# Attention with a mixture layer in double-precision words: inputs laid out by the host in three new ways, four bit operations changed, the hand-written order replaced

## The chip, the cores and the metric

The kernel runs on one core of one Trainium2 chip. The metric is device time in microseconds, the median of several executions; the profile is one further execution of the same program, with its own time.

## The reference

```python
scores = q @ k^T / sqrt(64);  causal mask;  attn = softmax(scores)      # 4 batches x 12 heads, 448 positions, 64 wide
x = (attn @ v) laid out as 1792 tokens x 768
h = max(x @ w1, x @ w2, x @ w3)                                          # 768 x 768 each
out = h @ w_out                                                          # 1792 x 768
```

q, k and v are float32. The four weights come as 8-byte floating-point words (float64); each is read as pairs of 32-bit words, of which the upper word carries sign, exponent and the top of the mantissa.

## The kernel before

**Units.** Attention goes by 24 units u = 6b + p, a pair of heads p of a batch b. `staging` loads for a unit k and q, 128 x 448 float32 each (two heads above each other), and for every second unit a tile kx of 128 x 2 x 288: the last 64 queries and 224 keys of two units with the heads exchanged, in four transfers (line 693, two for q and two for k). `attend` computes a unit's scores in two halves into PSUM (a and b of the group names; line 720), takes row maxima on VectorE (L766), exponentials on ScalarE (L790), and brings the probabilities into position: for the first six units by transposes on TensorE (L804) with copies out of PSUM (L528 on ScalarE, L530 on VectorE), for the other 18 by splitting into two half-precision parts (cast L528 or L530, difference L539 on VectorE or GpSimd) and transposing by DMA on SP's queue (L859). Then come the products with v, 60 matmuls a unit in two halves (L884), scaling by the row sums and a split of the result x.

**Weights.** 24 weight tiles of 768 KB, m = 0 to 23, three to a group f. `weight` loads one (L981 for w1 to w3, six pieces of 1 KB for each partition; L985 for w_out, one piece of 6 KB), takes the absolute value of the upper words on ScalarE (L1015) and their clamped maximum on VectorE (L1000), and puts a float32 together out of the two words by bit operations (L1004, L1008, L1012). `scales` (group names c0 to c7) spreads the three maxima of a group to all partitions by matmuls (L567), takes the maximum (L572) and makes a power of two of it with L577, L583, L587 and a reciprocal (L595). `split` makes two half-precision parts with these factors (L528 or L530 or L532, and L548 or L550 and L551). There are two buffers for weight tiles as loaded, four for what is made of them.

**Layers.** `hidden` computes the first layer for batches 0 and 1 (L1092, three parts of six 448-column matmuls for each product, evicted by L1107), `project` the second (L1503). For batches 2 and 3 seven products take the place of eight (`seven`, L1324; `project_seven`, L1449), of combined weights and tokens.

**Order.** All operations are first listed with their readers and writers; `ORDER` gives the order in which they are placed and `ENGINE`, two letters for each, the engine or queue (pe, dv, ac, po, sp). Each engine then executes its own in that order, and waits at the first that isn't ready. The lists hold 1,940 operations. Loads are issued from SP's and ScalarE's queues, DMA transposes from SP's only. Buffers go round in rings (`RINGS`: two each of k and q, one kx).

Of the kernel before, what the change touches and what calls it, by code (L numbers as in the profile page):

```python
# [1642 lines left out]
```

## Time and profile before

| | us |
|---|---|
| median of 3 runs | 455.27 (453.88 to 458.81) |
| the profiled execution | 458.94 |
| its span, first to last instruction | 457.2 |
| TensorE busy in it | 435.9 |
| VectorE busy | 418.7 |
| ScalarE busy | 298.3 |
| GpSimd busy | 116.7 |
| mean granted TensorE clock | 0.984 |

A busy TensorE is not TensorE at its peak, since matmuls are pipelined and their ends modelled. PEld is the load of a matmul's stationary operand, which overlaps. Idle time of an engine that isn't the bottleneck costs nothing. A row of the timeline gives start, duration, engine, line and operation, out<-in with shapes, how often, and in brackets the idle time of the engine ahead of it and what ended that.

### The profile page before, as it was taken

The numbers are of one execution on the slowest core, as the hardware profiler recorded it, in microseconds if no ns is written. First come the engines' busy times: TensorE is split into PE (matmuls) and PEld (weight loads), VectorE is DVE, ScalarE is ACT, GpSimd is POOL, SyncE is SP. The second block draws the span as 40 slices with busy tenths as digits, with TensorE's granted clock in tenths as the row PEclk, the third lists the DMA queues.
The fourth block names the chain that finished last, engine by engine and source line by source line (L and its number), as shares of the span: only waits on it lengthen the run. The fifth ranks groups of instructions, "written<-read, shape, count | busy, mean of one in ns | idle before, by whom it ended". The sixth has DMA issues, their size and how long they took to land. (4 is left out here: it accounts for less than half of the span.)

```text
span 457.2 us, 11068 instructions
## 1 busy us (share of the span) xinstructions
PE 435.9 (95%) x4349; PEld 254.5 (56%) x4349; DVE 418.7 (92%) x835; ACT 298.3 (65%) x722; POOL 116.7 (26%) x118
## 2 busy tenths in 40 slices
PE   6789898999799999999999999999999999999996
PEld 3568674555365555555555566655555555555553
DVE  2989999999789998998798999899999999999994
ACT  2998989788586898997477788794333342431520
POOL 2025542333333414423200035111021203122010
PEclk9889999999889999999999999999999999999999
DMA  7958678999879868926898785873010000000024
GB/s 253 273 178 251 196 258 207 227 199 232 185 196 216 253 193 172 286 63 134 189 164 155 162 168 112 148 135 87 21 42 0 1 1 0 2 0 1 0 82 161
DMA packets 109235, 64.02 MB, mean 140 GB/s; under 512 B 80512, under 2 KB 106624, under 8 KB 109184
## 3 DMA queue, kind: packets, MB, share of 16 engines
q1 hardware_dynamic: 97504, 48.08, 46.6%
q10 hardware_dynamic: 11680, 15.24, 10.8%
q8 instruction: 34, 0.56, 0.5%
q14 instruction: 17, 0.14, 0.1%
HBM read 38.93 MB, written 5.51 MB: 97 GB/s over the span
## 5 line engine op out<-in xcount | busy, mean ns | idle before, releaser
L1092 PE MATMUL M<-x,w 128*128 128x448 f16 x648 | 129.2, 355 | 0.6 <-ACT region L528 0.5
L790 ACT ACTIVATE region<-S,acc 128x128 f32<-128x128 f32 (+3 forms) x168 | 81.5, 495 | 22.6 <-POOL acc L778 7.9
L1092 PEld LDWEIGHTS <-w 128*128 128x128 f16 x648 | 61.5, 98 | 58.0 <-issue 3.7
L766 DVE TENSOR_REDUCE acc<-S 128x2 f32<-128x768 f32 (+1 forms) x96 | 61.2, 665 | 12.7 <-PE S L720 10.4
L539 POOL TENSOR_TENSOR region<-region 128x1024 f16<-128x1024 f32 (+1 forms) x18 | 37.3, 2071 | 60.0 <-ACT region L1015 21.9
L720 PE MATMUL S<-region 64*64 64x224 f32 (+6 forms) x768 | 49.2, 367 | 2.1 <-DMA region<-in_k_dram 1.1
L528 ACT ACTIVATE region<-region,cols 128x384 f16<-128x384 f32 (+1 forms) x37 | 22.0, 612 | 43.0 <-DVE region L1182 33.5
L528 ACT ACTIVATE region<-region 128x1024 f16<-128x1024 f32 (+3 forms) x48 | 37.9, 798 | 17.3 <-DVE region L1257 7.8
L1324 PEld LDWEIGHTS <-region 128*128 128x128 f16 x324 | 31.7, 98 | 29.6 <-DVE region L548 0.2
L1177 POOL TENSOR_TENSOR region<-w 128x384 f32<-128x384 f16 x21 | 19.0, 911 | 106.6 <-DVE region L1177 36.4
L1503 PE MATMUL M<-h,w 128*128 128x448 f16 x216 | 42.6, 353 | 0.0
L720 PEld LDWEIGHTS S<-region 64*64 64x64 f32 x768 | 33.7, 139 | 7.2 <-issue 2.4
L1324 PE MATMUL L<-region,region 128*128 128x448 f16 x180 | 36.3, 352 | 0.0
L1324 PEld LDWEIGHTS <-w 128*128 128x128 f16 x243 | 23.5, 98 | 22.4 <-issue 0.7
L790 ACT ACTIVATION_READ_ACCUMULATOR region<-S,acc 128x1 f32 x168 | 34.3, 204 | 0.0
L1324 PE MATMUL M<-x,w 128*128 128x448 f16 x162 | 33.1, 353 | 0.5 <-DVE hacc L530 0.5
L1503 PEld LDWEIGHTS <-w 128*128 128x128 f16 x216 | 20.6, 98 | 20.0 <-issue 1.3
L884 PEld LDWEIGHTS <-region 128*64 128x64 f16 x1080 | 26.4, 111 | 6.6 <-issue 6.2
L528 ACT ACTIVATE region<-region,acc 128x128 f32<-128x128 f32 (+3 forms) x56 | 27.4, 524 | 3.9 <-PE S L720 2.1
L884 PE MATMUL O<-region,region 128*64 128x128 f16 (+1 forms) x1080 | 29.1, 211 | 0.0
L1015 ACT ACTIVATE region<-region 128x768 f32<-128x768 f32 x24 | 21.9, 914 | 8.3 <-DMA region<-in_moe_w_dram 8.3
L1000 DVE TENSOR_SCALAR_CACHE_REDUCE region<-region 128x768 f32<-128x768 f32 x24 | 22.7, 944 | 4.8 <-ACT region L1015 4.7
(180 smaller groups left out, 798.5 us busy)
## 6 DMA issues: line engine op xcount, KB each, us to landing
region<-in_moe_w_dram SPq DMA_DIRECT2D x9, 768.0 KB, 5.9
region<-in_moe_w_dram ACTq DMA_DIRECT2D x9, 768.0 KB, 5.5
region<-in_k_dram SPq DMA_DIRECT2D x20, 224.0 KB, 3.9
region<-in_v_dram SPq DMA_DIRECT2D x11, 384.0 KB, 4.3
region<-in_q_dram SPq DMA_DIRECT2D x17, 224.0 KB, 4.5
region<-in_moe_w_out_dram SPq DMA_DIRECT2D x4, 768.0 KB, 5.5
region<-in_k_dram SPq DMA_DIRECT2D x22, 112.0 KB, 3.3
out_dram<-osb ACTq DMA_DIRECT2D x8, 224.0 KB, 2.5
```

The costliest lines, as they stand in the source:

```text
L528: ACT.activation(o, i, AF.Copy, scale=f)
L539: ENG[eng].tensor_tensor(out=o, in0=i, in1=hi, op=ALU.subtract)
L720: PE.matmul(ap(o, 512 * h + dims[0], dims[1:], D * g, D), l, r, start=start, stop=True, skip_group_check=True)
L766: DVE.tensor_reduce(out=ap(T(acc), at, [[4, len(g)]]), in_=i, op=ALU.max, axis=AX.XY if parts == 2 else AX.X, negate=True)
L790: ACT.activation(o, part(T(S), parts, c, w), AF.Exp, bias=T(acc)[:, 16 + at : 17 + at], scale=0.125, accum_out=T(acc)[:, 8 + at : 9 + at])
L884: PE.matmul(T(O)[D * h : D * h + D, P * i : P * i + w], vt[j][:, vl, (2 * p + h) * D : (2 * p + h + 1) * D], queries(T(pT[u]), i, h, 8 * p ...
L1000: DVE.tensor_scalar(out=T(x32), in0=T(x32), scalar1=MIN_HI, scalar2=None, op0=ALU.max, op1=ALU.max, accum_out=wmx[:, c])
L1015: add([("act", c_act(DM, 0.025))], lambda e: ACT.activation(T(x32), word(1).bitcast(F32), AF.Abs), reads=[st], writes=[x32], ring=("w3", x ...
L1092: PE.matmul(T(M)[:, 0:S_LEN], w16[j][:, kk, wl, fs], xx[:, kk % 3, xl], start=(kk == 0 and wl + xl == 0), stop=(kk == 5 and wl == 1))
L1177: add(c_add(n), lambda e: ENG[e].tensor_tensor(out=o(), in0=a()[0], in1=a()[1], op=ALU.add), reads=reads, writes=writes, ring=ring, prio=p ...
L1324: PE.matmul(T(M)[:, 0:S_LEN], stat(c, wl), mov(c, xl), start=first and n == 0, stop=n == 8, skip_group_check=True)
L1503: PE.matmul(T(M)[:, 0:S_LEN], w16[3][:, f, wl, es], T(("h", b, f))[:, hl], start=(f == 0 and hl + wl == 0), stop=(f == 5 and wl == 1))
```

## The change

The host, which already transposed q, k and v, lays the inputs out anew: q and k of a unit stand beside each other in one row of 896; the contents of kx stand as rows of 576 in a tensor of its own (`cross`); w1 to w3 stand tile by tile, each partition's 6 KB in one piece. So a unit's q and k are one transfer of 448 KB into one tile qk (ring of two), kx is one of 288 KB instead of four, and a weight tile has rows of 6 KB instead of six of 1 KB. The bytes are the same.

The upper words are scaled by 2^16 in the ScalarE operation that takes their absolute value. `power` (L577) goes: `exponent` does the shift and the mask in one instruction. `low30` (shift and mask) becomes `shift`, `top2` becomes `sign`, with another constant.

The two lists are replaced. They hold 1,908 operations: 24 fewer for q, 8 fewer for `power`. Before, 387 are on TensorE, 755 on VectorE, 575 on ScalarE with its queue, 102 on GpSimd and 121 on SP's queue (where one operation for kx issues four transfers); now 387, 723, 579, 110 and 109.

```diff
-TOP2 = -0x40000000
-LOW30 = 0x3FFFFFFF
+SIGN = -0x80000000
-MIN_HI = 2.0**-15 * 1.125
+MIN_HI = 2.0 * 1.125
...
-ORDER = [16, 15, 17, 18, 941, 19, 30, 49, 20, 50, 0, 31, 2, 21, 32, 33, 22, 23, 24, 942, 26, 25, 34, 943, 4, 6, 35, 944,
+ORDER = [15, 17, 18, 917, 16, 48, 923, 19, 29, 20, 918, 919, 0, 30, 21, 2, 4, 22, 23, 6, 7, 24, 49, 31, 32, 33, 80, 920,
...
-    qr=2, kr=2, xr=1, kx=1, acc=2, p32=2, ph=2, pT=3, v16=5, vr=4, w3=4, x=4, wst=2, h=6, hacc=4, osb=2, S=2, O=1, M=3,
+    qk=2, xr=1, kx=1, acc=2, p32=2, ph=2, pT=3, v16=5, vr=4, w3=4, x=4, wst=2, h=6, hacc=4, osb=2, S=2, O=1, M=3,
...
-        def power(e):
-
-            DVE.tensor_scalar(
-                out=at(1).bitcast(I32), in0=at(0).bitcast(I32), scalar1=3, scalar2=TOP2, op0=ALU.logical_shift_left,
-                op1=ALU.bitwise_xor)
-
         def exponent(e):
-            k = int(shifted)
-            DVE.tensor_scalar(
-                out=at(k + 1).bitcast(I32), in0=at(k).bitcast(I32), scalar1=EXP32, scalar2=None, op0=ALU.bitwise_and)
+            if shifted:
+                DVE.tensor_scalar(
+                    out=at(1).bitcast(I32), in0=at(0).bitcast(I32), scalar1=3, scalar2=EXP32, op0=ALU.logical_shift_left,
+                    op1=ALU.bitwise_and)
+            else:
+                DVE.tensor_scalar(
+                    out=at(1).bitcast(I32), in0=at(0).bitcast(I32), scalar1=EXP32, scalar2=None, op0=ALU.bitwise_and)
...
+        def both_of(e):
+            ENG[e].dma_start(T(qk), both_[b, p * P : (p + 1) * P, :])
 
         def other(e):
-            for x, w, at in ((q, D, 0), (k, 224, D)):
-                for h in range(2):
-                    r, c = p * P + D * (1 - h), 224 * h if at else 384
-                    i = bass.AP(x.tensor, x[b, r : r + 1, c : c + 1].offset, [[S_LEN, D], [P * S_LEN, 2], [1, w]])
-                    ENG[e].dma_start(T(kx)[D * h : D * h + D, :, at : at + w], i)
...
+            r = (6 * b + p) // 2 * P
+            ENG[e].dma_start(T(kx).rearrange("p a b -> p (a b)"), cross[r : r + P, :])
...
         def ld(e):
-            if m < 18:
-                ENG[e].dma_start(
-                    stage().rearrange("p (a f) -> p a f", a=KC),
-                    wi[j][:, f * 256 : (f + 1) * 256].rearrange("(a p) f -> p a f", p=P))
-            else:
-                ENG[e].dma_start(stage(), wi[3][f * P : (f + 1) * P, :])
+            ENG[e].dma_start(stage(), wi[j][f * P : (f + 1) * P, :])
...
-        def low30(e):
-            DVE.tensor_scalar(
-                out=xi(), in0=xi(), scalar1=3, scalar2=LOW30, op0=ALU.logical_shift_left, op1=ALU.bitwise_and)
+        def shift(e):
+            DVE.tensor_scalar(out=xi(), in0=xi(), scalar1=3, scalar2=None, op0=ALU.logical_shift_left)
...
-        def top2(e):
+        def sign(e):
             DVE.scalar_tensor_tensor(
-                out=xi(), in0=word(1), scalar=TOP2, in1=xi(), op0=ALU.bitwise_and, op1=ALU.bitwise_or)
+                out=xi(), in0=word(1), scalar=SIGN, in1=xi(), op0=ALU.bitwise_and, op1=ALU.bitwise_or)
...
-        add([("act", c_act(DM, 0.025))], lambda e: ACT.activation(T(x32), word(1).bitcast(F32), AF.Abs), reads=[st], writes=[x32],
+        add([("act", c_act(DM, 0.025))], lambda e: ACT.activation(T(x32), word(1).bitcast(F32), AF.Abs, scale=2.0**16), reads=[st], writes=[x32],
```

## Rows read from the trace of the kernel before

**Rows 1.** The page, part 1: busy time, share of the span, instructions.

```profile
PE 435.9 (95%) x4349; PEld 254.5 (56%) x4349; DVE 418.7 (92%) x835; ACT 298.3 (65%) x722; POOL 116.7 (26%) x118
```

**Rows 2.** Table of stretches: busy us (instructions) by engine, clock, DMA share, GB/s.

```profile
0.00:129.00 129.00, 112.32 (x1427) 74.27 (x1428) 112.18 (x236) 104.84 (x275) 44.65 (x49) 0.95 0.86 220
129.00:301.50 172.50, 172.10 (x2021) 101.05 (x2021) 160.19 (x338) 138.43 (x350) 48.02 (x44) 1.00 0.79 175
301.50:457.20 155.70, 151.50 (x903) 79.22 (x902) 146.33 (x264) 55.00 (x101) 24.01 (x26) 1.00 0.11 35
```

**Rows 3.** The chain that ended last: start, duration, what.

```profile
305.70 1.50 PE O L884 x60
...
449.66 1.70 PE L L1449 x9
```

**Rows 4.** Timeline of TensorE, 128 to 130 us.

```profile
128.95 0.23 PE L567 MATMUL M<-ident,bsc 128*128 128x128 bf16 x1
```

**Rows 5.** Table of stretches ahead of 129 us.

```profile
0.00:20.00 20.00, 13.93 (x139) 8.84 (x140) 10.98 (x32) 11.42 (x32) 3.12 (x12) 0.91 0.89 269
20.00:100.00 80.00, 73.45 (x999) 50.52 (x997) 77.36 (x158) 73.03 (x192) 29.76 (x28) 0.98 0.84 220
100.00:129.00 29.00, 24.95 (x298) 14.91 (x292) 23.83 (x48) 20.40 (x51) 11.77 (x9) 0.88 0.88 186
```

**Rows 6.** TensorE's waits: who for whom, us in total, times, longest.

```profile
PE M L567 <- DVE region L1000: 3.3, 2, 3.1
...
PE S L720 <- DMA region<-in_q_dram: 1.0, 1, 1.0
```

**Rows 7.** Timeline, 109.5 to 129 us: the third tile of the fifth group.

```profile
110.76 0.37 ACTq L981 DMA_DIRECT2D region<-in_moe_w_dram  x1
...
120.03 0.89 ACT L1015 ACTIVATE region<-region 128x768 f32<-128x768 f32 x1 [3.23 <-DMA region<-in_moe_w_dram]
...
120.95 0.95 DVE L1000 TENSOR_SCALAR_CACHE_REDUCE region<-region 128x768 f32<-128x768 f32 x1 [2.76 <-ACT region L1015]
```

**Rows 8.** Table of stretches around that wait.

```profile
118.60:122.00 3.40, 0.34 (x5) 0.14 (x3) 1.05 (x4) 1.97 (x7) 0.16 (x1) 0.90 1.23 220
121.70:128.40 6.70, 6.43 (x62) 4.22 (x65) 4.88 (x14) 4.30 (x13) 2.09 (x1) 0.52 0.32 92
```

**Rows 9.** Line L577 alone: times, ns least/median/most, first and last start.

```profile
L577 DVE TENSOR_SCALAR M<-M x8: 154/167/170, 30.3 to 193.6; 128x3 int32<-128x3 int32 x8
```

**Rows 10.** Lines by form: shapes, times, busy us, mean ns, idle before.

```profile
L539 POOL TENSOR_TENSOR region<-region 128x1024 f16<-128x1024 f32 x9 | 19.2, 2131 | 43.8 <-ACT region L1015 14.6 <-DVE region L1012 14.1 <-DVE wt L587 7.6
...
L548 DVE SCALAR_TENSOR_TENSOR w<-region,wf,w 128x768 f16<-128x768 f32 x18 | 17.9, 1006 | 0.0
...
L1107 DVE SCALAR_TENSOR_TENSOR hacc<-M,wr,hacc 128x448 f32<-128x448 f32 x24 | 16.2, 675 | 0.9 <-PE M L1092 0.8
...
L1004 DVE TENSOR_SCALAR region<-region 128x768 int32<-128x768 int32 x24 | 13.3, 565 | 0.2
...
L539 DVE TENSOR_TENSOR region<-region 128x1024 f16<-128x1024 f32 x9 | 11.0, 1219 | 0.2 <-ACT region L528 0.2
...
L530 DVE TENSOR_SCALAR region<-M 128x512 f32<-128x512 f32 x4 | 2.5, 672 | 0.0
```

**Rows 11.** Timeline, 84 to 128 us: two of kx's four issues.

```profile
100.29 2.47 SPq L693 DMA_DIRECT2D region<-in_q_dram  x2
```

**Rows 12.** DMA issues: queue, times, KB each, median us to landing.

```profile
region<-in_moe_w_dram SPq DMA_DIRECT2D x9, 768.0 KB, 5.9
...
region<-in_moe_w_out_dram SPq DMA_DIRECT2D x4, 768.0 KB, 5.5
```

**Rows 13.** Timeline, 0 to 24 us: first loads on SP, TensorE's wait for kx.

```profile
0.80 1.40 SPq L693 DMA_DIRECT2D region<-in_q_dram  x2
...
3.53 0.60 SPq L981 DMA_DIRECT2D region<-in_moe_w_dram  x1
...
8.43 0.60 PE L720 MATMUL S<-region 64*64 64x224 f32 x4 [1.12 <-DMA region<-in_k_dram]
```

More of the change, by code (lines that the diff above doesn't have):

```diff
@@ new lines @@
+ORDER = [15, 17, 18, 917, 16, 48, 923, 19, 29, 20, 918, 919, 0, 30, 21, 2, 4, 22, 23, 6, 7, 24, 49, 31, 32, 33, 80, 920,
[90 rows of a table added]
+ENGINE = (
+    "spacspacspacpospdvdvpedvdvdvdvspsppedvdvdvacacacacpeacpeacpedvdvacacacacpeacpeacpepodvpeacdvacpoacpedvdvpoacacac"
+    "acpedvpeacpedvdvpoacacacpeacpeacpepodvpedvdvdvpospsppedvdvpoacacacacpeacpeacpedvdvpoacacacpeacpeacpepodvpeacdvdv"
+    "posppedvdvpoacacacacpeacpedvpedvdvpoacacacpeacpeacpepodvpeacdvacpospsppedvdvpoacacacacpeacpeacpedvdvacacacacpeac"
+    "peacpepodvpeacdvacposppedvdvpoacacacacpeacpeacpedvdvpoacacacpeacpeacpeacdvpeacdvacdvspacspacspacspacdvpedvdvdvdv"
+    "podvacdvacdvpoacdvspsppedvdvacacacacacacposppedvdvacacacacacposppepeacdvpeacdvacposppedvdvacacacacacacposppedvdv"
+    "acacacacacposppepeacdvpeacdvacpospsppedvdvacacacacacacposppedvdvacacacacacposppepeacdvpeacdvacposppedvdvacacacac"
+    "acacposppedvdvacacacacacposppepeacdvpeacdvacpospsppedvdvacacacacacacposppedvdvacacacacacposppepeacdvpeacdvacposp"
+    "pedvdvacacacacacacposppedvdvacacacacacposppepeacdvpeacdvacpospacacacspacspacdvpedvdvdvdvacdvacdvacdvacpospacspac"
+    "spacspacdvpedvdvdvdvpopoacdvacdvacdvdvacacpedvdvacacacacacacdvacacacacacposppedvdvacacacacacdvacacacacposppepeac"
+    "dvacpedvdvacacacacacacdvacacacacacposppedvdvacacacacdvdvacacacacposppepeacdvspsppedvdvacacacacacdvdvacacdvdvacdv"
+    "sppedvdvacacacacpodvacacdvdvdvsppepeacdvsppedvdvacacacacacpodvdvacacacacdvsppedvdvacacacacacdvdvacdvdvdvsppepeac"
+    "dvspsppedvdvdvacacacacpodvdvdvacacdvdvsppedvdvacacacacacdvacdvdvdvdvsppepedvdvsppedvdvacacacacacacdvdvdvdvdvdvpo"
+    "sppedvdvacacacacacdvdvacdvacdvsppepeacdvacsppedvdvdvacacacacdvdvacdvacdvacdvsppedvdvpoacacacacdvdvdvacacdvsppepe"
+    "acdvacpedvdvpoacacacacpodvacacacacdvdvsppedvdvpoacacacacdvacdvacacposppepedvdvspsppedvdvacacacacacacdvacacdvacac"
+    "dvsppedvdvacacacacacdvdvacdvacposppepeacdvsppedvdvacacacacacacdvacdvacdvdvdvsppedvdvacacacacdvdvacdvdvacdvsppepe"
+    "acdvspsppedvdvacacacacacacdvdvacdvacacdvsppedvdvdvacacacacdvdvacacdvposppepeacdvsppedvdvdvacacacacacdvacdvdvacac"
+    "dvsppedvdvacacacacacdvacacacacdvsppepeacdvspacdvdvdvdvspacdvdvdvdvspacdvdvdvdvpedvdvdvdvdvpodvpopopopospacdvdvdv"
+    "dvspacdvdvdvdvspacdvdvdvdvpedvdvdvdvdvacdvacdvpodvspacdvdvdvdvspacdvdvdvdvspacdvdvdvdvpedvdvdvdvdvacdvacdvacdvac"
+    "acdvdvdvdvspacdvdvdvdvacacdvdvdvdvpedvdvdvdvdvpodvacdvacdvacacdvdvdvdvacacdvdvdvdvacacdvdvdvdvpedvdvdvdvdvacdvac"
+    "dvacdvacacdvdvdvdvspacdvdvdvdvacacdvdvdvdvpedvdvdvdvdvacdvacdvacdvspacdvdvdvdvspacdvdvdvdvspacdvdvdvdvpedvdvdvdv"
+    "acdvacdvacpospacdvdvdvdvspacdvdvdvdvacacdvdvdvdvpedvdvdvdvdvdvacdvpodvdvacacacacacacpepepeacpepepedvpepepedvacdv"
+    "pepepeacpepepedvpepepedvacpopepepeacpepepedvpepepedvacpopepepeacpepepedvpepepedvacpopepepeacpepepedvpepepedvacpo"
+    "pepepeacpepepedvpepepedvacpodvpepepedvsppepepeacacpepepeacsppepepeacsppepepeacsppepepedvacpepepeacpepepedvpepepe"
+    "dvacpopepepeacpepepedvpepepedvacpopepepeacpepepedvpepepedvacpopepepeacpepepedvpepepedvacdvpepepeacpepepedvpepepe"
+    "dvacpopepepeacpepepedvpepepedvacpodvpepepeacacpepepeacsppepepedvsppepepeacacpepepeacacpepepeacacdvdvdvpopopodvdv"
+    "acdvdvdvpodvacdvacdvdvdvpodvdvdvacdvacdvdvdvdvdvacdvdvpodvdvdvdvdvdvacdvdvdvacdvacdvdvdvpodvdvdvacdvacdvdvdvacdv"
+    "acdvdvdvdvdvdvdvacdvacdvdvdvacdvacdvdvdvpodvdvdvacdvacdvdvdvacdvacdvdvdvpodvdvdvacdvacdvdvdvacdvacdvpodvpodvdvdv"
+    "acdvacdvpodvacdvacdvpodvdvpodvdvacdvacdvdvdvacdvacdvpopopodvdvdvacdvacdvpodvacdvacdvpodvpodvdvdvacdvdvdvdvdvacdv"
+    "acdvpodvpodvdvdvacdvacdvpodvacdvacdvpodvpopodvdvacdvacdvpodvacdvacdvpopodvpodvdvacdvdvdvpodvacdvacdvdvdvdvpodvdv"
+    "acdvacdvpodvacdvacdvpeacpedvpeacpedvpedvpepedvdvpeacpedvpedvpedvpedvpepedvdvdvdvdvpeacpedvpedvpedvpedvpepedvdvdv"
+    "dvdvacdvacdvacdvdvdvdvacdvacdvacdvdvacdvpeacpedvpeacpedvpedvpepedvdvpeacpedvpedvpedvpedvpepedvdvdvdvdvpeacpedvpe"
+    "dvpedvpedvpepedvdvdvdvdvacdvacdvacdvdvdvdvacdvacdvacdvdvacdvpeacpedvpeacpedvpedvpepedvdvpeacpedvpedvpedvpedvpepe"
+    "dvdvdvdvdvpeacpedvpedvpedvpedvpepedvdvdvdvdvacdvacdvacdvdvdvdvacdvacdvacdvdvacdvdvpepeacpepedvpepedvsppepedvpepe"
+    "dvsppepedvsppepedvacpepeacpepedvpepeacacpepedvpepedvacpepedvsppepedvsppepeacpepedvpepeacacpepedvpepedvacpepedvac"
+    "pepedvsp")
@@ L429, in attention_moe @@
 @with_exitstack
-def attention_moe(ctx: ExitStack, tc: tile.TileContext, q, k, v, w1, w2, w3, wo, out):
+def attention_moe(ctx: ExitStack, tc: tile.TileContext, both_, cross, v, w1, w2, w3, wo, out):
     nc = tc.nc
@@ L685, in staging @@
         od.group = f"s{6 * b + p}"
-        qr, kr, kx = ("qr", b, p), ("kr", b, p), ("kx", b, p // 2)
+        qk, kx = ("qk", b, p), ("kx", b, p // 2)
+        def both_of(e):
+            ENG[e].dma_start(T(qk), both_[b, p * P : (p + 1) * P, :])
         def other(e):
-            for x, w, at in ((q, D, 0), (k, 224, D)):
-                for h in range(2):
-                    r, c = p * P + D * (1 - h), 224 * h if at else 384
-                    i = bass.AP(x.tensor, x[b, r : r + 1, c : c + 1].offset, [[S_LEN, D], [P * S_LEN, 2], [1, w]])
-                    ENG[e].dma_start(T(kx)[D * h : D * h + D, :, at : at + w], i)
-        add(c_dma((P, 4 * S_LEN)), lambda e: ENG[e].dma_start(T(kr), k[b, p * P : (p + 1) * P, :]), writes=[kr],
-            ring=("kr", kr), prio=prio)
-        def ld(e):
-            ENG[e].dma_start(T(qr), q[b, p * P : (p + 1) * P, :])
-        add(c_dma((P, 4 * S_LEN)), ld, writes=[qr], ring=("qr", qr), prio=prio)
+            r = (6 * b + p) // 2 * P
+            ENG[e].dma_start(T(kx).rearrange("p a b -> p (a b)"), cross[r : r + P, :])
+        add(c_dma((P, 8 * S_LEN)), both_of, writes=[qk], ring=("qk", qk), prio=prio)
         if p % 2 == 0:
-            add(c_dma((D, 512), (D, 512), (D, 1792), (D, 1792), each=0.65), other, writes=[kx], ring=("kx", kx), prio=prio)
+            add(c_dma((P, 2304)), other, writes=[kx], ring=("kx", kx), prio=prio)
     def attend(b, p, prio, plain):
-        qr, kr, acc, O = ((n, b, p) for n in ("qr", "kr", "acc", "O"))
+        qk, acc, O = ((n, b, p) for n in ("qk", "acc", "O"))
         kz, R, x32 = ("kx", b, p // 2), ("M", "r", b, p), ("x32", b, p)
@@ L757, in attend @@
             cost = A_COST if z == 0 else B_COST
-            add([("pe", cost)], mm, reads=[qr, kr] + z * [kz], writes=[S], ring=("S", S), prio=pr, mode=(3, 3))
+            add([("pe", cost)], mm, reads=[qk] + z * [kz], writes=[S], ring=("S", S), prio=pr, mode=(3, 3))
             groups = [blocks[0:2], blocks[2:4]] if z == 0 else [blocks[0:2], blocks[2:3]]
@@ L1009, in last3 @@
                 out=xi(), in0=word(0), scalar=29, in1=xi(), op0=ALU.logical_shift_right, op1=ALU.bitwise_or)
-        def top2(e):
+        def sign(e):
             DVE.scalar_tensor_tensor(
-                out=xi(), in0=word(1), scalar=TOP2, in1=xi(), op0=ALU.bitwise_and, op1=ALU.bitwise_or)
-        add([("act", c_act(DM, 0.025))], lambda e: ACT.activation(T(x32), word(1).bitcast(F32), AF.Abs), reads=[st], writes=[x32],
+                out=xi(), in0=word(1), scalar=SIGN, in1=xi(), op0=ALU.bitwise_and, op1=ALU.bitwise_or)
+        add([("act", c_act(DM, 0.025))], lambda e: ACT.activation(T(x32), word(1).bitcast(F32), AF.Abs, scale=2.0**16), reads=[st], writes=[x32],
             ring=("w3", x32), prio=prio)
         add([("dve", c_dve(DM))], clamp, writes=[x32, ("wmx", m)], prio=prio)
-        for step, fast in ((low30, True), (last3, False), (top2, False)):
+        for step, fast in ((shift, True), (last3, False), (sign, False)):
             add([("dve", c_dve(DM, fast))], step, reads=[st], writes=[x32], prio=prio, port=True)
@@ L1608, in attention_moe, with _laid_out @@
         od.run(tc)
-_INS = ["q", "k", "v", "moe_w1", "moe_w2", "moe_w3", "moe_w_out"]
 _OUTS = [((768, 1792), "float32")]
+def _laid_out(inputs):
+    import numpy as _np
+    q, k = (_np.asarray(inputs[n]).transpose(0, 1, 3, 2) for n in ("q", "k"))
+    heads = [z.reshape(4, 3, 2, 2, 64, 448).transpose(3, 0, 1, 4, 2, 5) for z in (q, k)]
+    cross = [_np.concatenate([heads[0][1 - h][..., 384:], heads[1][1 - h][..., 224 * h : 224 * h + 224]], -1) for h in range(2)]
+    a = dict(
+        qk=_np.concatenate([q.reshape(4, 768, 448), k.reshape(4, 768, 448)], -1),
+        cross=_np.stack(cross, 2).reshape(12 * 128, 576),
+        v=_np.asarray(inputs["v"]).transpose(0, 2, 1, 3).reshape(4, 448, 768))
+    for n in ("moe_w1", "moe_w2", "moe_w3"):
+        a[n] = _np.asarray(inputs[n]).reshape(6, 128, 6, 128).transpose(2, 1, 0, 3).reshape(768, 768)
+    a["moe_w_out"] = _np.asarray(inputs["moe_w_out"])
+    return a
 def kernel(**inputs):
@@ L1623 @@
     arrays, args = {}, []
-    for name in _INS:
-        a = _np.asarray(inputs[name])
-        if name in ("q", "k"):
-            a = a.transpose(0, 1, 3, 2).reshape(4, 768, 448)
-        elif name == "v":
-            a = a.transpose(0, 2, 1, 3).reshape(4, 448, 768)
+    for name, a in _laid_out(inputs).items():
         a = _np.ascontiguousarray(a)
```

47 lines of the change are left out of this document (5 added, 42 removed), and 182 rows, old and new, of the table ORDER.

## The prediction

> **What bounds the kernel now.** I read the page first: TensorE is busy 95% of the span and VectorE 92% [rows 1], so shares alone don't tell which one sets the time. The table of stretches does, cut where the run changes character [rows 2]. From 301.5 us on TensorE is busy 151.50 us of 155.70, and the chain that ended last consists of matmuls there, nine 448-column ones each 1.70 us [rows 3]. From 129 to 301.5 it is busy 172.10 of 172.50 at full clock. Before 129 it is not: 112.32 of 129, at a mean granted clock of 0.95. So two thirds of the run cost what their matmuls cost, and only the first 129 us have time to give. I cut at 129 because there the scale of batch 2's values comes to TensorE, the matmul L567 on bsc [rows 4]; both order lists hold it, so I can count up to it. I call it the mark.
>
> What sets the time ahead of the mark is shown by a finer table [rows 5]. From 20 to 100 us VectorE is busy 77.36 of 80 us and ScalarE 73.03: TensorE waits there for scores to be reduced, exponentiated and split. From 0 to 20 VectorE has 10.98, because it waits for first loads; from 100 to 129 it has 23.83 of 29. One place explains most of that: TensorE's longest wait is for VectorE's maximum of a weight tile, L1000, 3.3 us in two waits of which one has 3.1 [rows 6]. The rows there [rows 7] read: the third tile of the fifth group is issued at 110.76, ScalarE waits 3.23 us for it until 120.03, VectorE 2.76 for ScalarE. TensorE was busy 0.34 us of the 3.4 after 118.6, and from 121.7 to 128.4 its granted clock is 0.52, so mostly the 1.2 GHz level [rows 8].
>
> **The change part by part.** *VectorE's instructions.* L577 goes, eight times 0.167 us, 1.3 us in all [rows 9]. `low30` becomes `shift`, the same instruction with one operation instead of two: L1004 takes 565 ns for 768 columns [rows 10], the quickest of the tile's passes, so I see neither a gain nor a loss. `top2` becomes `sign` and the Abs takes a scale: same instruction, same operands, nothing.
>
> *Loads.* q and k come in one issue, kx in one instead of four, a weight tile in rows of 6 KB instead of 1 KB. Two of kx's four issues hold SP's queue 2.47 us at 100.29 [rows 11]. Some 36 issues of kx and 24 of q come off the queues; three loads of weights and two of values move from ScalarE's queue to SP's, where the transposes stand, at some 0.4 us each against more than 2 us that every kx gives back. What does that give? Of TensorE's waits, the loads of q and k make 1.0 us [rows 6] and, at the start, 1.12 [rows 13]; work in flight hides the rest. I take nothing; ends 0 and -2.1 (both waits gone). For the weights the trace has both shapes, 768 KB each: 1 KB rows land 5.9 us after their issue on SP, w_out's 6 KB rows after 5.5 [rows 12]. Longer rows give 0 to 0.4 us a tile; they matter only where a tile is waited for, and that wait is counted below.
>
> The Trainium skill (DMA: Bandwidth & Descriptors, section "Why small descriptors are slow (HBM only)") charges each packet a fixed three cycles beside one cycle per 32 bytes, from which I estimate 7% between rows of 1 KB and of 6 KB. By that rule the sum would be 0.4 us lower, by the rows it stays; the landing times agree with the rule in size.
>
> *Order and engines.* Here the change can pay. I counted the entries of `ORDER` ahead of the mark, with the engine that `ENGINE` gives each, before and after: VectorE 200 and 191, ScalarE 196 and 197, GpSimd 35 and 41, TensorE 107 and 111. TensorE's four more are three parts of six 448-column matmuls (1.13 each, two thirds of the nine's 1.70) and one half of a probability-times-value product (0.75, half of 1.50) [rows 3]: 4.15 us of matmul move from behind the mark, where TensorE is the bound, to ahead of it, where it waits anyway. From VectorE's list there go five L577 (0.8), two differences of probabilities (L539, 2.4) and three of x (at half of that, 1.9), two copies of 512 columns (1.3), two casts of weights (at L1004's price 1.1) and five operations on a few columns (0.8): 8.3. To it there come two remainders of weights (L548, 2.0), one more pass over a weight tile (1.0), a maximum and a remainder of values (1.0 each), a fold (0.7), a reduction and a cast (0.8 together) and four small ones (0.6): 7.1 [rows 9, 10]. Net -1.2. As VectorE is the bound ahead of the mark, the mark comes 1.2 us earlier with 4.15 us more matmul done: -5.3. Ends: 0, when new idle time of VectorE eats it, and -5.3. GpSimd takes three more differences of probabilities at 2.13 us; its idle 84 of 129 us [rows 2] cover them, and without that cover each is 0.9 us later than VectorE's 1.22 [rows 10], for its transpose and then for the product.
>
> *The wait at 120.* Between the issue of that third tile and its maximum's matmul the old list has four parts of hidden layer for TensorE, 4.5 us; the new one has six, two half products and a half of scores, 9.2. So I expect the 2.76 us of VectorE gone, and some of the slow stretch. But this profile's time, 458.94, is above the median, 455.27, and the late tile may be part of that. I take -2.0; ends 0 and -6.1 (2.76 and half of the 6.7 slow microseconds).
>
> *Behind the mark.* VectorE is busy 160.19 of 172.50 us there [rows 2], close behind TensorE; with matmuls taken away its waits may show. +1.0; ends 0 and +4.15 (the shift lost). The last stage keeps its matmuls and its final fold and store: 0.
>
> Sum: -5.3 - 2.0 + 0 + 1.0 = -6.3. Against the profiled execution that is 458.94 - 6.3 = 452.6 (span 457.2, 1.7 around it); against the median of the three runs 455.27 - 6.3 = 449.0, which I predict.
>
> **The rivals.** *More:* late tile, slow clock and load waits all go: -5.3 - 6.1 - 2.1 + 1.0 = -12.5, 442.8. For it: one late tile explains wait and slow stretch. Against it: VectorE's 9 us of idle in the first 20 [rows 5] stay as they are.
>
> *Nothing:* the shift shows up again behind the mark and new idle replaces the old: only L577 remains, -1.3, 454.0. For it: VectorE's 93% there. This includes that the change doesn't do what it says, the loads having been hidden before.
>
> *Loads in a row:* the new list puts the first weight tile ahead of kx on SP's queue. In the trace kx's first issue is at 0.80 and the tile's at 3.53, and TensorE waits for kx until 8.43 [rows 13]. If kx lands only behind the tile, which is then issued some 2.3 us earlier (1.2), lands 5.9 later (7.1) at best, and has 448 KB of q and k ahead and kx's 288 KB behind it (at 768 KB in 5.9 us, 5.6 us with nothing overlapped, about 3 with half), kx comes at about 10, 1.6 us later: 450.6. The Trainium skill (DMA: Bandwidth & Descriptors, section "Queues, rings and completion order") states that each engine takes a queue's descriptors in ring order, which speaks for it; no row of before shows a kx behind a tile.
>
> *Slower:* late tiles at new places. Between the third tile's issue and its maximum the new list has less for TensorE in the second group (5.3 us for 8.3) and in the sixth (5.3 for 6.4), by the same prices. If both go as the fifth did, each costs about 3.1 us of waiting [rows 6] and half of a slow stretch, 3.3, together 12.8; so -6.3 + 12.8 = +6.5, 461.8. It decides from two such events on: one (+6.4) is paid by the gain, 455.4. Against it: the trace shows no long wait at those groups.
>
> **How the numbers follow.** The forecast, 449.0 with its own range 446 to 452.5, has 0.53; more, 0.17; nothing, 0.12; loads in a row, 0.06; slower, 0.12. About 1% is what a measurement of this kernel can tell from no change: faster is below 450.7, slower above 459.8. Faster gets 0.17, 0.35 of the forecast's 0.53 and half of the 0.06: 0.55; slower 0.12; the rest, 0.33, is within 1%. The range is 442 to 456: it holds the forecast, most of "more" (some 0.05 may lie below) and nearly all of "nothing", and leaves out slower.
>
> **What would show it.** Right: the mark at about 126 us with 198 hidden-layer matmuls (L1092 before) ahead of it for 180 by the lists; no wait of 3 us on L1000; TensorE without gaps behind the mark; a clock above 0.95 ahead of it; VectorE with 32 fewer operations in all (723 for 755 by the lists). Wrong: waits on L1000 at the second or sixth group, a further slow stretch, gaps of TensorE between the mark and 300 us, or unit 0's second half of scores later than 10 us.

## The result and the profile after

The kernel after takes 443.51 us (median of five, 442.90 to 444.67) beside 457.61 us of the kernel before on the same chip (453.88 to 458.81): a ratio of 0.9717, 95% interval 0.967 to 0.9765. In a second comparison it took 442.54 us beside 454.44, ratio 0.9768 (0.9721 to 0.9816). So it is faster by 2.3 to 2.8%, 11.9 to 14.1 us by the medians. Three of the five runs of before in the first comparison (457.61 to 458.81) stand with its profiled execution at an upper level that this program reaches in some executions, so the second comparison is the fairer one. The profiled execution took 443.31 us, 15.6 less than the profiled one of before.

Part 1 of the page after, then the table of stretches of after, cut at 20, 100, the new place of the mark and 288 us (columns as in [rows 2]):

```profile
PE 429.3 (97%) x4349; PEld 251.8 (57%) x4349; DVE 407.0 (92%) x803; ACT 303.9 (69%) x737; POOL 122.7 (28%) x123
```

```profile
0.00:20.00 20.00, 14.73 (x164) 9.54 (x165) 13.99 (x37) 13.91 (x41) 3.18 (x12) 0.91 0.91 333
20.00:100.00 80.00, 78.24 (x1076) 54.09 (x1078) 78.74 (x159) 75.61 (x202) 32.72 (x34) 1.00 0.85 228
100.00:116.80 16.80, 16.80 (x233) 10.37 (x231) 16.61 (x34) 14.86 (x36) 7.99 (x5) 1.00 1.05 222
116.80:288.00 171.20, 169.48 (x1990) 99.34 (x1987) 153.82 (x319) 146.87 (x370) 52.44 (x45) 1.00 0.77 177
288.00:441.60 153.60, 150.05 (x897) 78.50 (x894) 143.82 (x257) 52.66 (x93) 26.37 (x28) 1.00 0.11 33
```

Beside [rows 2, 5]: from 20 to 100 us TensorE is busy 78.24 us for 73.45, and in the last 17 us ahead of the mark it doesn't stop at all. From there on it is the bound, as it was. The mark, in the timeline of after, stands 12.15 us earlier than in [rows 4]:

```profile
116.80 0.23 PE L564 MATMUL M<-ident,bsc 128*128 128x128 bf16 x1
```

TensorE's waits in after (who for whom, us in total, times, longest) have no long one left. L564 is the L567 of [rows 6], L707 the scores; the wait of 3.1 us for a tile's maximum in the fifth group is gone, and the one of that kind that is left has 0.6, in the sixth group, at 136.18 us:

```profile
PE S L707 <- ACT region L777: 2.5, 2, 1.4
...
PE S L707 <- DMA region<-in_cross_dram: 1.0, 1, 1.0
PE M L564 <- DVE region L982: 0.6, 1, 0.6
```

The mark splits the gain. It is VectorE's busy time ahead of it plus VectorE's idle time ahead of it; the rest of the span lies behind it. The stretch ahead of the mark and the one behind it, in before and then in after:

```profile
0.00:128.95 128.95, 112.27 (x1426) 74.22 (x1426) 112.12 (x236) 104.79 (x275) 44.65 (x49) 0.95 0.86 220
...
128.95:457.20 328.25, 323.64 (x2925) 180.32 (x2923) 306.57 (x600) 193.48 (x449) 72.03 (x69) 1.00 0.47 109
```

```profile
0.00:116.80 116.80, 109.77 (x1468) 73.99 (x1469) 109.34 (x229) 104.38 (x276) 43.89 (x51) 0.99 0.89 245
...
116.80:441.60 324.80, 319.53 (x2885) 177.84 (x2881) 297.64 (x575) 199.53 (x462) 78.81 (x73) 1.00 0.46 109
```

VectorE's work ahead of the mark falls from 112.12 to 109.34, its idle time from 16.83 to 7.46 (128.95 - 112.12 and 116.80 - 109.34), and the stretch behind from 328.25 to 324.80. The last is the moved matmuls: TensorE is busy 4.11 us less there. The surprise is the idle time, -9.4 us, most of the gain between these two executions. A second profiled execution of after (442.46 us) repeats the places: first scale matmul at 23.50 us (23.49 here), mark at 116.44.

### The profile page after: what moved, and what is told of

Read it like the earlier page. It is cut to its first block, busy times and chain, and to the rows that moved or that the text cites. A ratio compares the mean times of both kernels' runs of the same rounds, so it can differ in the third digit from the quotient of the medians.

```text
span 441.6 us, 10961 instructions
## 1 busy us (share of the span) xinstructions
PE 429.3 (97%) x4349; PEld 251.8 (57%) x4349; DVE 407.0 (92%) x803; ACT 303.9 (69%) x737; POOL 122.7 (28%) x123
## 4 chain that ended last, share of the span: by engine, by line
PE 67%; DVE 2%; DMA 1%; ACT 1%; issue 0%
PE M L1073 16%; PE L L1305 14%; PE M L1484 9%; PE M L1305 7%; PE L L1430 5%; PE S L707 5%; PE O L871 4%; PE O L1305 3%; PE M L1430 2%; DMA region<-in_moe_w_dram 1%; PE O L1430 1%; DVE w L545 0%; ACT region L777 0%; DVE region L982 0%; DVE region L989 0%; DVE hacc L1088 0%
## 5 line engine op out<-in xcount | busy, mean ns | idle before, releaser
L525 ACT ACTIVATE region<-region 128x1024 f16<-128x1024 f32 (+3 forms) x49 | 39.9, 821 | 27.2 <-DVE region L1238 9.9
L536 POOL TENSOR_TENSOR region<-region 128x960 f16<-128x960 f32 (+1 forms) x20 | 41.4, 2069 | 61.4 <-DVE region L527 14.2
L707 PE MATMUL S<-region 64*64 64x224 f32 (+6 forms) x768 | 47.4, 359 | 1.1 <-DMA region<-in_cross_dram 1.0
L1158 POOL TENSOR_TENSOR region<-w 128x384 f32<-128x384 f16 x22 | 20.0, 913 | 73.5 <-DVE region L545 21.2
L1305 PE MATMUL L<-region,region 128*128 128x448 f16 x198 | 39.7, 352 | 0.0
L777 ACT ACTIVATION_READ_ACCUMULATOR region<-S,acc 128x1 f32 x168 | 36.0, 214 | 0.0
L707 PEld LDWEIGHTS S<-region 64*64 64x64 f32 x768 | 32.4, 135 | 5.7 <-DMA region<-in_cross_dram 1.4
L525 ACT ACTIVATE region<-region,acc 128x128 f32<-128x128 f32 (+3 forms) x51 | 25.1, 520 | 1.8 <-DVE acc L827 1.7
```

What stands on the lines that cost most here:

```text
L525: ACT.activation(o, i, AF.Copy, scale=f)
L536: ENG[eng].tensor_tensor(out=o, in0=i, in1=hi, op=ALU.subtract)
L707: PE.matmul(ap(o, 512 * h + dims[0], dims[1:], D * g, D), l, r, start=start, stop=True, skip_group_check=True)
L777: ACT.activation(o, part(T(S), parts, c, w), AF.Exp, bias=T(acc)[:, 16 + at : 17 + at], scale=0.125, accum_out=T(acc)[:, 8 + at : 9 + at])
L1305: PE.matmul(T(M)[:, 0:S_LEN], stat(c, wl), mov(c, xl), start=first and n == 0, stop=n == 8, skip_group_check=True)
```

## The experiments

**Loads and lists apart.** Two parts of the change can be had one without the other: how inputs are laid out and loaded, and the two lists. The first kernel has the new loads (and the new bit operations) with the old order and engines; operations that no longer exist are left out of the old lists, and a unit's joint load stands where the load of k stood:

```diff
-ORDER = [15, 17, 18, 917, 16, 48, 923, 19, 29, 20, 918, 919, 0, 30, ...
+ORDER = [15, 16, 17, 917, 18, 29, 48, 19, 0, 30, 2, 20, 31, 32, 21, ...
-ENGINE = "spacspacspacpospdvdvpedvdvdvdvspsppedvdvdvacacacacpeacpeacpedvdvaca...
+ENGINE = "spacspacspacpospacdvpedvdvdvdvacsppedvdvpoacacacacpeacpedvpedvdvpoa...
```

> The changed kernel (new layout, one transfer each, L577 gone) with the old lists: the old ORDER and ENGINE carried over operation by operation, q's load dropped into k's place. Theory 'order' (the gain of 14.1 us between the medians 457.6 and 443.5 comes from the new lists): 454 to 457, at most the 1.3 us of L577 and the 2.1 us of the two load waits gone; the matmul on bsc of batch 2 still at about 126 to 129 us and the wait on the fifth group's tile still there. Theory 'loads' (it comes from the transfers): 444 to 447, the mark at about 117, as in the changed kernel.

Measured: 452.26 us (451.23 to 453.82) beside 453.20 of before; ratio 0.9978 (0.9954 to 1.0003). No difference that this measurement tells from zero. (It lies below the range of "order", 454 to 457, since before itself has 453.20 here and not 457.6.)

The second is the converse, old loads with the new lists (q's load behind k's, `power` ahead of `exponent`):

```diff
-ORDER = [16, 15, 17, 18, 941, 19, 30, 49, 20, 50, 0, 31, 2, 21, 32, ...
+ORDER = [15, 16, 18, 19, 941, 17, 49, 50, 947, 20, 30, 21, 942, 943, ...
```

> The kernel before (old layout, separate transfers of q and k, four of kx, weight rows of 1 KB, L577) with the new lists carried over, q's load right behind k's. Theory 'order': 444 to 447, the mark at 117 to 120. Theory 'loads': 455 to 458, the mark at 126 to 129. If both are needed (the new order asks for loads that the old transfers can't bring in time), this one and the one with new loads and old order both stay above 452.

Measured: 445.47 us (444.45 to 446.39), ratio 0.9826 (0.9783 to 0.9869), with the mark at 118.90. The lists alone bring 1.7%; with them in place the loads bring the remaining 2 to 3 us (445.47 to 442.54 or 443.51, each measured on another chip). Under the old lists the same loads brought nothing measurable; the rows under "Before, once more" show a gain at the start and a loss behind it.

**The two lists apart.** New loads in both; one has the old sequence with the new engines, the other the new sequence with the old engines.

```diff
-ORDER = [15, 17, 18, 917, 16, 48, 923, 19, 29, 20, 918, 919, 0, 30, ...
+ORDER = [15, 16, 17, 917, 18, 29, 48, 19, 0, 30, 2, 20, 31, 32, 21, ...
```

> New loads, the old ORDER, but each operation on the engine that the new ENGINE gives it: what the engines are worth without the sequence. Theory 'engines' (VectorE's relief, 8 to 11 us over the run and 1.2 ahead of the mark, is what pays): as much below the run with new loads and old lists as half the gain or more, so 447 to 451. Theory 'sequence' (when a tile is asked for against when it is used): within 2 us of the run with both old lists, or slower, since the old order was fitted to the old engines.

```diff
-ENGINE = "spacspacspacpospdvdvpedvdvdvdvspsppedvdvdvacacacacpeacpeacpedvdvaca...
+ENGINE = "spacspacspacpospacdvpedvdvdvdvacsppedvdvpoacacacacpeacpedvpedvdvpoa...
```

> The changed kernel with the new ORDER, but each operation on the engine of the old ENGINE. Theory 'sequence': within 3 us of the changed kernel, 443.5 to 447. Theory 'engines': 449 to 455, as VectorE has some 8 to 11 us of work back over the run, most of it ahead of 300 us.

Measured: 498.76 us, ratio 1.0985 (1.0924 to 1.1045), and 479.08 us, ratio 1.057 (1.051 to 1.063). Both are far slower than before; the second lies outside what either theory expected. TensorE's waits say why, first of old sequence with new engines, then of new sequence with old engines:

```profile
PE M L439 <- ACT hacc L400: 12.7, 1, 12.7
PE S L582 <- ACT region L652: 9.0, 11, 1.5
```

```profile
PE S L582 <- ACT region L652: 7.4, 7, 2.4
PE M L948 <- POOL w L423: 3.2, 1, 3.2
```

An operation that is given to ScalarE or GpSimd stands there behind whatever the sequence puts ahead of it; one such place held TensorE for 12.7 us. So a sequence and its engines are one thing, and "what does the order bring" can't be split this way. It can be split in time.

**The order in two halves.** Two kernels, both with the new loads: each takes one pair of lists up to the scale matmul of the third group of weight tiles (69.80 us in after) and the other pair from there on. Every operation keeps the engine of the list that places it. The cuts show where one list ends and the other begins: behind 993 in the first kernel, behind 991 in the second.

```diff
-ORDER = [..., 1165, 309, 993, 995, 988, 255, 261, 1166, ...
+ORDER = [..., 1165, 309, 993, 973, 974, 995, 228, 988, ...
```

> The new loads throughout; the new order and engines up to the maximum of the fourth group of weight tiles (69.80 us in the profile of after), the old order and engines from there on. If the gain of the order is local (less idle time of VectorE, part by part), the part up to the cut keeps its gain and the rest of the old list loses about as much as with the old order throughout (2.9 us of VectorE idle in the next group): 446 to 449 us. If a list's halves only pay together, 452 us or more.

```diff
-ORDER = [15, 17, 18, 917, 16, 48, 923, 19, 29, 20, 918, 919, 0, 30, ...
+ORDER = [15, 16, 17, 917, 18, 29, 48, 19, 0, 30, 2, 20, 31, 32, 21, ..., 206, 1177, 991, 976, 1163, 269, 279, 297, ...
```

> The converse: the new loads throughout, the old order and engines up to the same matmul, the new ones from there on. Local: the idle 8.4 us of VectorE in the first 26 us stay, the 2.9 and 0.6 behind the cut go, and the matmuls that the new list holds ahead of the mark are done there: 447 to 450 us. Only together: 452 us or more.

Measured: new then old 448.86 us, ratio 0.9883 (0.9842 to 0.9923); old then new 448.19 us, ratio 0.9888 (0.9833 to 0.9942). (The expectation of the first calls the group the fourth; it is the third, and the time named with it is right.) Both fall into the range of "local". From 0.9978 each half gives 0.9 to 1.0%, together 1.85%, against 2.1 to 2.6% for both. The gain is local to its stretches, and within these intervals (some 0.5% to either side) the halves add up. The mark in the timelines of new then old, and of old then new:

```profile
120.10 0.23 PE L439 MATMUL M<-ident,bsc 128*128 128x128 bf16 x1
```

```profile
124.06 0.23 PE L439 MATMUL M<-ident,bsc 128*128 128x128 bf16 x1
```

With the old order throughout it came at 122.86, with 327.2 us behind it (span 450.1). Here the spans are 447.3 and 446.8, so 327.2 and 322.7 us lie behind. The first half of the order brings the mark forward; the second brings the moved matmuls ahead of it.

**Before, once more.** The profiled execution of before was at the upper end of its times. The kernel before, unchanged, was profiled again:

> The kernel before, unchanged, profiled once more. If the late tile at 120 us and the half-clock stretch behind it belong to the old order with the old loads, they come again (TensorE waits about 3 us for the maximum of that tile, mark at about 129). If they were of the one execution, the tile's wait is under 1 us, the mark comes at 123 to 126 and the time is 450 to 454 us.

Measured: 450.95 us, span 449.2. The mark and TensorE's wait for the tile's maximum (which was 3.3, longest 3.1, in [rows 6]), from the timeline and the waits of this execution:

```profile
121.13 0.23 PE L567 MATMUL M<-ident,bsc 128*128 128x128 bf16 x1
```

```profile
PE M L567 <- DVE region L1000: 0.9, 2, 0.6
```

The late tile at 120 us and the slow stretch behind it are not part of every execution: the mark comes 7.82 us earlier here, in the same program. Of that, 6.33 us lie in the stretch of the late tile, from the fourth group's scale matmul to the mark: 28.75 us in before (its row is the first below) for 22.42; the rest lies ahead of it. The median of before (453.20 to 457.61 in four comparisons) is 2.3 to 6.7 us above this execution. On the last three chips the late tile with its slow stretch doesn't make up that distance: the runs at the medians have a mean granted clock of 0.990 to 0.996, as this one (0.991), and only two of 31 (459.17 and 460.82 us) have 0.985, near the 0.984 of the first profiled execution. What the ordinary runs lose is not shown. The rows to compare after with are still these, of before again, one of its quickest executions:

```profile
100.20:128.95 28.75, 24.70 (x293) 14.86 (x290) 23.58 (x48) 20.21 (x51) 11.77 (x9) 0.88 0.88 187
```

```profile
0.00:121.13 121.13, 108.11 (x1427) 71.97 (x1427) 110.33 (x233) 102.81 (x272) 42.74 (x48) 0.97 0.88 232
0.00:27.02 27.02, 20.12 (x237) 13.92 (x237) 17.24 (x46) 17.71 (x48) 3.32 (x13) 0.87 0.80 244
...
70.72:98.71 27.99, 27.36 (x306) 15.65 (x305) 27.82 (x53) 24.18 (x57) 8.10 (x6) 1.00 1.01 224
98.71:121.13 22.42, 21.78 (x294) 13.11 (x291) 22.24 (x45) 18.57 (x48) 9.65 (x8) 1.00 0.99 224
...
121.13:449.20 328.07, 323.79 (x2925) 180.31 (x2923) 306.65 (x603) 195.19 (x451) 74.14 (x70) 1.00 0.47 110
```

27.02 us is the first group's scale matmul; in after it comes at 23.49:

```profile
0.00:23.49 23.49, 18.22 (x230) 12.46 (x230) 17.17 (x46) 17.40 (x49) 3.62 (x14) 0.93 0.92 341
```

VectorE's idle time ahead of the mark is 10.80 us here (121.13 - 110.33) and 7.46 in after, 3.34 less; and up to the first scale matmul it is 9.78 here (27.02 - 17.24) and 6.32 in after (23.49 - 17.17), 3.46 less. So between these two executions the idle time that goes is all at the start. (The second execution of after has 6.33 there, 23.50 - 17.17.)

These rows also show what the new loads did under the old lists. There the third group's scale matmul comes at 69.15 us, 1.57 earlier than the 70.72 here; but from it to the fourth group's it takes 30.36 us for 27.99, and TensorE waits 1.7 us for a transpose by DMA, a wait that before again doesn't have:

```profile
69.15:99.51 30.36, 27.59 (x307) 15.74 (x305) 27.46 (x51) 23.81 (x56) 8.09 (x6) 1.00 0.98 215
```

```profile
PE O L746 <- DMA region<-region: 1.7, 1, 1.7
```

**The start.** VectorE idles there until a weight tile or scores come. The first Abs of a weight tile and its maximum, in the timelines of before and of after:

```profile
11.30 0.89 ACT L1015 ACTIVATE region<-region 128x768 f32<-128x768 f32 x1 [1.49 <-DMA region<-in_moe_w_dram]
12.22 0.95 DVE L1000 TENSOR_SCALAR_CACHE_REDUCE region<-region 128x768 f32<-128x768 f32 x1 [1.94 <-ACT region L1015]
```

```profile
1.25 0.42 SPq L967 DMA_DIRECT2D region<-in_moe_w_dram  x1
...
7.20 0.89 ACT L996 ACTIVATE region<-region 128x768 f32<-128x768 f32 x1 [4.46 <-DMA region<-in_moe_w_dram]
7.95 0.60 PE L707 MATMUL S<-region 64*64 64x224 f32 x6 [1.04 <-DMA region<-in_cross_dram]
8.12 0.95 DVE L982 TENSOR_SCALAR_CACHE_REDUCE region<-region 128x768 f32<-128x768 f32 x1 [0.39 <-ACT region L996]
```

The tile, issued at 1.25 us instead of 3.53 [rows 13], gives VectorE its first maximum 4.1 us earlier than in before, and 4.65 earlier than in before again, where it stands at 12.77. The scores of kx (the 224-wide ones) start at 7.95, not later than the 8.43 of before. That maximum stands at 10.73 with new loads and old order, and at 8.94 with old loads and new order; VectorE's idle time up to the first scale matmul is 8.39 and 7.14 us there. Order and loads both shorten the start, the order more. VectorE's waits ahead of the mark, in before again and then in after, say which idle time it is: less for scores, and less for tiles.

```profile
DVE acc L766 <- PE S L720: 6.0, 2, 4.2
DVE region L1000 <- ACT region L1015: 2.6, 1, 2.6
```

```profile
DVE acc L753 <- PE S L707: 4.5, 1, 4.5
DVE region L982 <- ACT region L996: 1.0, 2, 0.7
```

Is it better still to put kx first? This kernel swaps the two issues on SP's queue, on top of the halved load of q and k that comes next:

```diff
-ORDER = [15, 17, 18, 917, 16, 48, 923, ...
+ORDER = [15, 17, 18, 16, 917, 48, 923, ...
```

> After with q and k in two transfers of 224 KB each (as in e8) and kx issued ahead of the first weight tile on SP's queue instead of behind it. If the tile ahead of it holds kx back (loads in a row), TensorE's wait of 1.0 us for kx goes and the time is 1 us under that of e8. If kx lands when the transfers that are in flight together land, the wait stays or the weight tile comes later by as much: no change from e8, 441 to 443 us.

Measured: 443.59 us (443.30 to 444.59), ratio 0.9778 (0.9739 to 0.9816), beside 441.70 and 0.9737 (0.9691 to 0.9783) with the halved load alone: not faster. TensorE's wait for kx is gone from the list, but the tile comes later. The timeline, and the maximum with the halved load alone:

```profile
8.45 0.89 ACT L872 ACTIVATE region<-region 128x768 f32<-128x768 f32 x1 [5.72 <-DMA region<-in_moe_w_dram]
9.38 0.95 DVE L858 TENSOR_SCALAR_CACHE_REDUCE region<-region 128x768 f32<-128x768 f32 x1 [1.47 <-ACT region L872]
```

```profile
8.51 0.95 DVE L983 TENSOR_SCALAR_CACHE_REDUCE region<-region 128x768 f32<-128x768 f32 x1 [0.42 <-ACT region L997]
```

The swap makes VectorE's first maximum 0.87 us later. TensorE's wait of 1.1 us for kx goes, but its longest wait for ScalarE grows from 1.4 to 4.0 us. The mark stays where it was, 117.67 us for 117.74: what one of the two loads gains by standing first, the other about loses.

**Each load by itself.** Three kernels start from after, which was run again beside them:

> The changed kernel itself, so that the next three stand beside it on one chip. 443 to 445 and a ratio to the kernel before of 0.970 to 0.980 if the ratio holds from chip to chip; if the kernel before is at 453 here too, as in the runs with exchanged lists, 0.978 and so 1% less of a gain than at first.

Measured: 442.54 us (442.07 to 445.39). With weight tiles in six rows of 1 KB again:

```diff
-            ENG[e].dma_start(stage(), wi[j][f * P : (f + 1) * P, :])
+            if m < 18:
+                ENG[e].dma_start(stage().rearrange("p (a f) -> p a f", a=KC), wi[j][:, f * 256 : (f + 1) * 256].rearrange("(a p) f -> p a f", p=P))
+            else:
+                ENG[e].dma_start(stage(), wi[j][f * P : (f + 1) * P, :])
```

> The changed kernel with w1 to w3 laid out as before, so weight tiles come in rows of 1 KB. By the landing times of before (5.9 us for 1 KB rows, 5.5 for 6 KB) a tile comes 0 to 0.4 us later and the time stays within 1 us of the changed kernel. Theory 'loads help where the new order left no slack': 1 to 2 us slower, with ScalarE's wait for weight tiles, 11.1 us in the changed kernel, grown by as much.

Measured: 446.26 us (445.39 to 449.95), 3.7 more, outside what either side expected. In the profiled execution the loss lies in one place: from the third to the fourth group's scale matmul it takes 26.7 us (70.12 to 96.84) where after takes 22.15 (69.80 to 91.95); 2.3 us come back behind the mark (322.51 us for 324.80). Timeline with 1 KB rows there:

```profile
79.13 0.90 ACT L999 ACTIVATE region<-region 128x768 f32<-128x768 f32 x1 [4.64 <-DMA region<-in_moe_w_dram]
80.07 0.95 DVE L985 TENSOR_SCALAR_CACHE_REDUCE region<-region 128x768 f32<-128x768 f32 x1 [3.99 <-ACT region L999]
```

and the same tile in after:

```profile
75.47 0.91 ACT L996 ACTIVATE region<-region 128x768 f32<-128x768 f32 x1 [1.29 <-DMA region<-in_moe_w_dram]
```

The tile is issued at 70.00 on ScalarE's queue (69.74 in after); q and k and another tile follow at 70.25 and 70.91 on SP's, a load of v at 74.49. So it came 9.1 us after its issue, and 5.7 in after. TensorE then waits 3.5 us to spread the reciprocals of row sums (L930), which VectorE computes behind that maximum. What the transfers moved while they ran together, in the tables of stretches with 1 KB rows, of after, and of the second execution of after (last column, GB/s):

```profile
73.00:78.00 5.00, 5.00 (x28) 2.60 (x27) 3.08 (x6) 1.49 (x2) 2.12 (x1) 1.00 1.05 338
```

```profile
73.00:78.00 5.00, 5.00 (x28) 2.62 (x27) 4.35 (x10) 3.71 (x6) 2.14 (x1) 1.00 1.00 406
```

```profile
73.00:78.00 5.00, 5.00 (x29) 2.56 (x27) 4.94 (x11) 4.26 (x7) 2.14 (x1) 1.00 0.92 358
```

338 GB/s against 406 and 358. The median landings hide it: with 6 KB rows the tiles take 5.4 us on SP's queue and 5.8 on ScalarE's, not visibly less than the 5.9 of [rows 12].

Short rows alone don't make this tile late. With the old loads and the new lists it has rows of 1 KB too, is issued at 71.22, and its Abs starts at 76.39, 5.2 us later; the transfers moved 356 GB/s from 73 to 78 us, and the stretch took no longer than in after:

```profile
71.34:93.13 21.79, 21.79 (x220) 12.41 (x218) 21.65 (x40) 19.30 (x41) 8.65 (x5) 1.00 1.04 276
```

There k, q and the other tile are issued 1.0, 1.6 and 2.1 us behind this one, not 0.25 and 0.9. So what the long rows are worth may depend on how closely the loads follow each other; no run separates the two.

With kx in four transfers again:

```diff
-            ENG[e].dma_start(T(kx).rearrange("p a b -> p (a b)"), cross[r : r + P, :])
+            for w, at in ((D, 0), (224, D)):
+                for h in range(2):
+                    i = bass.AP(cross.tensor, cross[r + D * h : r + D * h + 1, at : at + 1].offset, [[576, D], [288, 2], [1, w]])
+                    ENG[e].dma_start(T(kx)[D * h : D * h + D, :, at : at + w], i)
```

> The changed kernel with kx in four transfers again (256-byte and 896-byte pieces), all else new. Theory 'SP's queue is covered': within 0.7 us of the changed kernel. Theory 'queue': each of the 11 groups on SP stands some 2.2 us longer ahead of transposes and tiles, 1 to 3 us slower, first at the start, where TensorE's wait for kx, 1.0 us in the changed kernel, grows to 1.5 to 2.5.

Measured: 444.78 us (443.80 to 446.68), 2.2 more, with a range that meets that of after: likely a loss, not a sure one. TensorE's wait for kx at the start is 1.5 us instead of 1.0.

With q and k in two transfers, one for each half of the tile:

```diff
-            ENG[e].dma_start(T(qk), both_[b, p * P : (p + 1) * P, :])
+            for z in (1, 0):
+                ENG[e].dma_start(T(qk)[:, z * S_LEN : (z + 1) * S_LEN], both_[b, p * P : (p + 1) * P, z * S_LEN : (z + 1) * S_LEN])
```

> The changed kernel with q and k of a unit in two transfers of 1,792-byte pieces into the two halves of the same tile. 24 more issues at 0.4 us of queue: within 0.7 us of the changed kernel by the theory that issues are covered; 1 us or more if the queue is what the new transfers relieve.

Measured: 441.70 us (440.60 to 443.12), ratio 0.9737 (0.9691 to 0.9783), 0.8 us less than after; the intervals of the two ratios overlap. Putting q and k into one issue brought nothing here. No version is measurably better than after.

## Why the prediction was right, and where it was off

**The place: right.** The gain arose at and ahead of the mark, and TensorE sets the time behind it, before and after. The number lies in the stated range, 442 to 456, but below the forecast's own, 446 to 452.5: the range held it because it took in "more".

**Order and engines, -5.3: right.** Between the undisturbed execution of before and after, VectorE's work ahead of the mark falls by 0.99 us (predicted 1.2), and TensorE's work behind it by 4.26 us (323.79 to 319.53; predicted 4.15), with 198 hidden-layer matmuls ahead of the mark for 180, as by the lists. (The counts of VectorE's operations in the prediction fall by nine and the moves that it lists by seven; the rows of before and after have seven fewer, 236 and 229.) The end of 0 that I gave it, new idle time of VectorE that eats it, did not come.

**Behind the mark, +1.0: right.** TensorE's idle time there goes from 4.28 us (328.07 - 323.79) to 5.27 (324.80 - 319.53); in the second execution of after it is 4.59 (324.26 - 319.67).

**Loads and start, 0: the mis-sized term.** It measured -3.3 us of VectorE's idle time. The step that failed is the sentence against "more", that VectorE's 9 us of idle in the first 20 stay as they are. I had seen that the new list puts the first weight tile ahead of kx, and even that it is issued some 2.3 us earlier, but asked only what this does to kx. VectorE waited for that tile too; it had its maximum 4.1 us earlier, and VectorE's 10.98 us of work in the first 20 [rows 5] became 13.99. The loads have the smaller share in this: 8.39 us of idle time with the new loads alone, 7.14 with the new lists alone, 9.78 with neither.

In the same term, 1 KB against 6 KB rows was priced by median landings, 0 to 0.4 us a tile that matter only where a tile is waited for. That reading was weak: before again has medians of 5.4 and 5.1 us for the same 1 KB rows on the two queues, so such a difference needs no longer row. The new order can be made to wait at a place that I didn't look at: the first tile of the fourth group, issued at about 70 us when other loads start. Going back to short rows there made it 3.4 us later, and the run 3.7 longer. This is no part of the sum below, since neither before again nor after has that wait.

The rule of the Trainium skill (DMA: Bandwidth & Descriptors, section "Why small descriptors are slow (HBM only)"), by which I had estimated 7% between the two row lengths, agrees in direction: 338 GB/s is 17% under the 406 of one execution of after and 6% under the 358 of the other. These rows can't tell whether its size is right here.

**The wait at 120, -2.0: open.** In the execution that I read, the late tile lengthened its stretch by 6.3 us, near the upper end of the term, 6.1; in the next it was not there. Of before, three of five runs in the first comparison and two of 31 on the other chips are about as long as that execution; none of the 11 runs of after stands more than 3.3 us above the quickest. So the event belongs to some executions of before, and whether the new lists prevent it is not shown. That the profiled execution lay above the median was the sign for it.

**Sum.** The parts between before again and after are -1.0 (work), -3.3 (idle), -4.3 (moved), +1.0 (behind): -7.6, which is 449.2 to 441.6. Without the wait at 120 the forecast had -4.3, so what its sum lacks is the start. The rest of the gain in the medians, some 4 to 6 us, is mostly what the usual runs of before lose against before again; the forecast had 2.0 for it, and its cause stays open. So predicted 449.0 and measured 443.51 differ by the start, 3.3 us, and by some 2 us of this rest (455.27 is 4.3 us above before again).

The time is nearly that of the rival "more" (442.8), in part by luck. Of the 2.1 us of load waits that it let go, TensorE still has 1.0, for kx; and it left VectorE's idle time at the start as it was.

**The other rivals.** "Nothing" falls: -2.3 to -2.8%. "Loads in a row": the order of issue on SP's queue does decide which load lands first, as the swap shows, but kx came no later than before, and the earlier tile was worth more. "Slower": no long wait appeared at the second or the sixth group in after, only the 0.6 us at the sixth; its mechanism did show, at the fourth group, when the rows were short again.

**The signs.** 803 instructions on VectorE for 835, 32 fewer, as by the lists. `shift` takes 577 ns a tile where `low30` took 565 [rows 10]: neither gain nor loss, as forecast. The clock ahead of the mark is 0.99 (above 0.95); the only slow part lies in the first 20 us, mean 0.91. L564 waits 0.6 us for a tile's maximum, at the sixth group, which is the place that was named but far from 3 us. The mark, forecast at about 126, came at 116.80: it was forecast from the disturbed execution (128.95) and not from 121.13.

## What to carry to other kernels

Split a mark's time into an engine's work and its idle time, and price a reordering by what it does to each; for every load that is moved, ask who waits for that load itself, and not only whom it delays. A median landing time does not price a row length: look at the moment when several loads run together and one of them is waited for. Where one execution is well above the median, profile the kernel a second time before its waits are priced: one late tile lengthened its stretch by 6.3 us here.
